# A fourth output pair by Strassen, weights of two blocks side by side, and an inner Strassen in four units of the first feed-forward pass

## The chip, the cores and the metric

The kernel runs on one core of a Trainium2 chip. The core has a matrix engine (TensorE, PE in the profile, with its weight loads shown apart as PEld), a vector engine (VectorE, DVE), an activation engine (ScalarE, ACT), a general engine (GpSimd, POOL) and an engine that here only issues DMAs (SyncE, SP). Each runs its own list of instructions in order and waits on semaphores for the others. The metric is the device time of one execution in microseconds. The kernel before takes 712.45 us, the median of three runs (712.12 to 712.63).

## The reference

One transformer block on x of 2048 tokens by 1024, in bfloat16:

```
h   = x + linear_attention(layernorm(x), wqkv) @ wo      # 32 heads of 32
g   = layernorm(h) @ W_gate ;  u = layernorm(h) @ W_up   # 1024 -> 3584
out = h + (relu(g) * u) @ W_down                         # 3584 -> 1024
```

The linear attention has phi(t) = (t+1 where t>0, else exp(t)) + 1e-6 on queries and keys, a sum of k-transposed v per head, and a division by the summed keys.

## The kernel before, in words

Nearly every product is computed by Strassen's scheme in Winograd's form: a product of 2x2 blocks costs seven block products (P1 to P7) and a number of block sums. The sums of the weights (T1 to T4) and of the activations (S1 to S4) are made in fp16 by VectorE or GpSimd; partial results are forked from bank to bank of PSUM by ScalarE (`fk1`, `fk2`) or added while they are read out by VectorE.

The order of the work is written out by hand. Helpers append instructions to five lists, one for each engine; reads and writes of named buffers (`B_...`) become semaphore waits. So the place where a helper is called is the place of its instruction in its engine's queue, and a DMA that waits holds up every later DMA of the SP list.

**Output projection.** Tokens come in 16 tiles of 128. `a4_mm` computes one tile's product with wo directly: 16 matmuls of 128x512. `a4_h` adds the residual on VectorE and starts the tile's layer norm statistics on ScalarE and GpSimd; `a4_norm` normalises (ScalarE) and `a4_t` transposes by DMA into `hnT`. `o_group` computes a pair of tiles by Strassen: 28 matmuls of 128x512, six VectorE sums out of PSUM, and four sums of the transposed inputs (`o_sums`) before it. `NDIR = 10` tiles (0 to 9) go directly and pairs 5, 6 and 7 by Strassen. Tiles 0 to 7 are those of the first feed-forward pass. Tiles 8 and 9 have their residual placed in PSUM by ScalarE first (`a4_pre`), and ScalarE copies their result out. Between these matmuls stand the numerators of the attention (`a2_num`, called `nd` with its division): 12 of the 16 tiles' in this stage, with the rest before it. GpSimd makes the sums of wo, the first unit's T sums and the `o_sums`, one at a time, placed by `pq` and by the lists of the loop over `d`.

**Feed-forward.** There are two passes of 1024 tokens. A pass has 14 units (`ffn_unit`), even ones for the gate and odd ones for the up projection; a gate and an up unit together give four 128-wide columns of h. The unit's seven products are each 8 matmuls of 128x512 (two halves u, four steps each). P1 has an inner Strassen in most units (`R1` to `R7`, 14 matmuls of 128x256, with weight sums by `w_inner1`), done during the unit before. In the second pass alone P5 has one too (`M1` to `M7`, with weight sums `g5` by `w_inner` and activation sums `xs5` by `x_inner`). VectorE's list in a unit holds, in this order: the arguments `pre`, then `wina`, then `winb`, then the evacuations `c22`, `Ra` and `c12`, which release PSUM banks, then `tail`, then (up units) the products `h22` and `h12`. ScalarE's list takes `lna` and `lnb`: in the first pass these are the layer norm steps of the second pass's tokens (`late_steps`), two steps a unit. VectorE also makes in the first pass the sums of W_down (`wd_pair` in gate units, `wl_sums` in up units), stored to DRAM by SP; `load_wraw` reads the next raw pair; GpSimd makes four sums of raw W_down in each gate unit (`raw`, run as `mid`). `hh_pair` makes sums of h for the down projection.

**Weights.** A ring `wring` has six slots. A unit uses two: each load brings 1024 rows by 256 columns, in runs of 512 bytes; slot u belongs to half u.

**Down projection.** `down_pass` follows each feed-forward pass.

Of the kernel before, what the change touches and what calls it, by code (L numbers as in the profile page):

```python
# [132 lines left out]
def bass_sequential_preLN__linear_attn_block__glu_gated_reglu__prompt_kernel(  # L133
# [71 lines left out]
    with es:  # L205
# [22 lines left out]
        NDIR = 10  # L228
# [52 lines left out]
        c22 = RE[:, 2 * D:3 * D].rearrange("p (a b) -> p a b", b=SBW)  # L281
        c12 = RE[:, 3 * D:4 * D].rearrange("p (a b) -> p a b", b=SBW)
# [26 lines left out]
        Tring = RO[:].bitcast(f16).rearrange("p (s j k c) -> p s j k c", s=NTR, j=4, k=KH)  # L309
# [4 lines left out]
        wring = RWG[:].rearrange("p (s k c) -> p s k c", s=NWG, k=NDC)  # L314
# [253 lines left out]
        for i, st in enumerate(range(NDIR, NST)):  # L568
            if i < NHS:
                j = st % NHS  # L570
                hp_home[st] = hsb[:, j, :]
                over = [B_hs[j]]
            else:
                hp_home[st] = xo[:, i - NHS, :]
                over = [B_xo[i - NHS]]
            for b_ in B_hp[st]:
                b_.over = over
        hp_b = [b for st in B_hp for b in B_hp[st]]
        for b_ in B_D1:
            b_.over = B_xn + B_TWo[0::2] + B_hs + hp_b[0:2 * NHS]  # L580
# [14 lines left out]
        for b_ in B_hnE:  # L595
            b_.over = B_o + B_oT[0:NOE]
        for b_ in B_V:
            b_.over = B_hnE
        for b_ in flat(B_hh) + B_out2:
            b_.over = flat(B_xnT) + flat(B_pqT)  # L600
        ra_t = [B_TWo[1::2], flat(B_So), B_x2[TPP + NX2:], B_xo + hp_b[2 * NHS:]]
# [87 lines left out]
        def load_w_next():  # L689
# [5 lines left out]
            q, which = n_ - n_ % 2 + L % 2, n_ % 2  # L695
            i = L % NWG
            src = (wg_v if which == 0 else wu_v)[:, :, q * 2 * P:(q + 1) * 2 * P]
            dma(sl_w[i], wring[:, i, :, :], src, "ld_w_%d" % L, writes=[B_w[i]])
# [115 lines left out]
        def wd_pair(q):  # L814
# [17 lines left out]
            def three():  # L832
                add(wsum[:, :, 3, :], wb(1, 0), wsum[:, :, 1, :], B_wraw + bs(1), bs(3))
                for k in range(2):
                    dma(sl_ws[k], t_v[:, k, :, q // 2, :], wsum[:, k].rearrange("p o (h c) -> p (o h) c", c=HNW),
                        "st_wt_%d" % (q + k), reads=B_wsum[k], writes=[B_tscr[q + k]])
                    dma(sl_rw[k], r_v[:, 0, 2 * k:2 * k + 2, q // 2, :],
                        wraw[:, k, 1, NW:2 * NW].rearrange("p (h c) -> p h c", c=HNW), "st_rw_%d" % (q + k),
# [3 lines left out]
        def wl_sums(m):  # L842
# [28 lines left out]
            def last():  # L871
                addw(3, wr(1, 0), t_(1))
                dma(sl_lw[z], l_v[:, 4, :, m, :], lsw[:, z], "st_wm_%d" % m, reads=B_lsw[z], writes=[B_wscr[m]])

            def nxt():
                for q in (2 * m + NWR, 2 * m + NWR + 1):
                    if q < NPAIR:
                        load_wraw(q)
            raw = [lambda: addw(0, wr(0, 1), wr(0, 0)), lambda: addw(2, wr(1, 1), wr(0, 1)),
# [501 lines left out]
        def a4_mm(st, at):  # L1381
            k = st % NOT
            b, pre = a4_bank[st], st >= TPP
# [12 lines left out]
        def a4_pre(st):  # L1396
            b = a4_bank[st] = H_PAIRS[st % 2]
            if st >= TPP:
# [106 lines left out]
        def a4_h(st, mid, mid2):  # L1505
# [3 lines left out]
            if st < TPP:  # L1509
# [8 lines left out]
            if st >= TPP:  # L1518
                return
# [4 lines left out]
                                     "ln2_%d" % st)  # L1524
            mean()
            mid2()
            square()
            m_, r_, n_ = s2[:, ks, 0:1], s2[:, ks, 2:3], s2[:, ks, 4:5]
            PL.add("pool", lambda e: e.tensor_scalar(out=n_, in0=m_, scalar1=r_, scalar2=-1.0, op0=ALU.mult,
                                                     op1=ALU.mult),  # L1530
                   reads=[B_s2[ks][0], B_s2[ks][2]], writes=[B_s2[ks][4]], name="lnn_%d" % st)
# [72 lines left out]
        def t_sums(L, eng="dve"):  # L1604
            i = L % NWG
            k = L % NTR
            n = 1 if eng == "pool" else 2

            def wb(kk, h, u):
                return wring[:, i + u:i + u + n, kk * KH:(kk + 1) * KH, h * P:(h + 1) * P]  # L1610

            def tb(j, u):
                return Tring[:, k + u:k + u + n, j]

            def add(j, f0, f1, td):
                def go(u):
                    r = range(u, u + n)
# [1173 lines left out]
```

## Time and profile before

| | us |
|---|---|
| median of three runs | 712.45 |
| the profiled execution, its own time | 712.03 |
| its span, first to last instruction | 710.3 |
| TensorE busy | 701.9 |
| VectorE busy | 612.0 |
| ScalarE busy | 411.7 |
| GpSimd busy | 161.3 |

The granted TensorE clock is 1.000 over the whole span. TensorE's stages, by the trace: output projection from about 165.6 to 222.5, the first pass's units from there to about 390, its down projection to about 469, the second pass's units to about 632, its down projection to the end. A busy time is the time in which at least one instruction of the engine runs, so an engine that is busy 99% of a stage has no visible gap there. A few matmul records are missing from the trace; where one is missing, the trace shows "issue" for some 0.05 us and a step of two matmuls.

### The profile page before, as it was taken

What the parts mean: (1) busy time and instruction counts of PE and PEld (TensorE: products, weight loads), DVE (VectorE), ACT (ScalarE), POOL (GpSimd) and SP (SyncE); (2) the same over time, 40 slices, a digit from 0 to 9 for tenths busy, and PEclk for the clock granted to TensorE, in tenths of its full rate; (3) what the DMA queues carried; (4) which work ended last, traced back from release to release, by engine and by line L of the source; (5) the groups of instructions that cost most, each with busy time, mean ns of one, the idle gap of its engine ahead of it and who ended that gap; (6) DMA issues with size and microseconds to landing.
All of it is one profiled execution on the core that took longest, in us unless ns stands there. A gap on an engine that the chain in (4) does not pass through costs nothing.

```text
span 710.3 us, 13375 instructions
## 1 busy us (share of the span) xinstructions
PE 701.9 (99%) x5027; PEld 397.6 (56%) x5081; DVE 612.0 (86%) x982; ACT 411.7 (58%) x739; POOL 161.3 (23%) x234
## 2 busy tenths in 40 slices
PE   9999999999999999999999999999999999999998
PEld 4444444444444455555554658865555555568887
DVE  6988867899878899999998787888989988989996
ACT  4887667764973687878786411036666667651010
POOL 3221100114983223132312001321111110000331
PEclk9999999999999999999999999999999999999999
DMA  9852344015999799999898999998465644368996
GB/s 300 257 125 61 41 130 153 36 31 98 225 210 286 225 338 301 312 245 305 261 295 242 271 252 310 321 236 246 141 178 163 194 130 135 96 237 307 345 283 186
DMA packets 203537, 151.10 MB, mean 213 GB/s; under 512 B 54352, under 2 KB 180048, under 8 KB 203472
## 3 DMA queue, kind: packets, MB, share of 16 engines
q1 hardware_dynamic: 198480, 145.65, 70.5%
q0 software_dynamic: 4032, 3.67, 3.5%
q10 hardware_dynamic: 960, 0.92, 0.4%
q8 instruction: 40, 0.66, 0.4%
q14 instruction: 25, 0.20, 0.1%
HBM read 101.97 MB, written 36.18 MB: 194 GB/s over the span
## 4 chain that ended last, share of the span: by engine, by line
PE 92%; DVE 2%; issue 1%; ACT 1%; DVEq 0%
PE ps L886 92%; DVE RO L1618 0%; ACT RXH L926 0%; DVE RW L822 0%; DVE RAB L1752 0%; DVE RE L1752 0%; DVE RAB L1652 0%; DVE ps L1752 0%; ACT RX L966 0%; ACT RX L891 0%; ACT ps L891 0%; ACT RE L1296 0%; DVE RX L2019 0%; DVEq L118 0%
## 5 line engine op out<-in xcount | busy, mean ns | idle before, releaser
L891 ACT ACTIVATE ps<-ps 128x512 f32<-128x512 f32 (+1 forms) x265 | 134.4, 518 | 182.2 <-PE ps L886 138.3
L886 PE MATMUL ps<-RC,RO 128*128 128x512 f16 x616 | 147.0, 369 | 0.0
L886 PEld LDWEIGHTS ps<-RC,RO 128*128 128x128 f16 x616 | 60.1, 98 | 53.1 <-ACT ps L891 1.2
L886 PE MATMUL ps<-RC,RWG 128*128 128x512 f16 x320 | 80.9, 379 | 0.2 <-ACT ps L891 0.2
L891 ACT ACTIVATE RE<-ps 128x512 f32<-128x512 f32 (+3 forms) x106 | 64.2, 628 | 29.0 <-PE ps L886 12.7
L886 PE MATMUL ps<-RH,RWG 128*128 128x512 bf16 (+1 forms) x347 | 77.5, 348 | 0.1
L886 PE MATMUL ps<-RH,RO 128*128 128x512 bf16 (+1 forms) x228 | 59.3, 379 | 1.5
L1752 DVE TENSOR_TENSOR RE<-ps,RE 128x1024 bf16<-128x1024 f32 (+1 forms) x42 | 44.0, 1047 | 17.3 <-PE ps L886 17.2
L886 PEld LDWEIGHTS ps<-RH,RWG 128*128 128x128 bf16 x348 | 34.0, 98 | 35.2 <-ACT ps L891 0.2
L2028 POOL DMA_DIRECT2D out_dram<-RX x20 | 18.0, 1270 | 151.3 <-DVE RX L2019 100.3
L886 PE MATMUL ps<-RW,RAB 128*128 128x256 f16 (+3 forms) x351 | 51.5, 298 | 0.2
L886 PE MATMUL ps<-RAB 128*128 128x512 bf16 (+3 forms) x235 | 49.6, 347 | 0.2
L886 PEld LDWEIGHTS ps<-RC,RWG 128*128 128x128 bf16 (+1 forms) x320 | 30.0, 98 | 33.8 <-ACT ps L891 5.1
L886 PEld LDWEIGHTS ps<-RW,RAB 128*128 128x128 f16 (+1 forms) x354 | 34.5, 98 | 13.8 <-DVE RAB L1464 0.5
L2019 DVE TENSOR_TENSOR RE<-ps,RE 128x512 f32<-128x512 f32 x46 | 31.6, 687 | 12.0 <-PE ps L886 11.4
L1764 ACT ACTIVATE RAB<-RAB 128x1024 bf16<-128x1024 bf16 x28 | 29.5, 1055 | 19.0 <-DVE RAB L1752 19.0
L1752 DVE TENSOR_TENSOR RAB<-ps,RE 128x1024 bf16<-128x1024 f32 x28 | 34.2, 1222 | 7.0 <-PE ps L886 6.4
L1618 DVE TENSOR_TENSOR RO<-RWG 128x1024 f16<-128x1024 bf16 x54 | 39.4, 729 | 0.0
L1752 DVE TENSOR_TENSOR RAB<-RAB,RE 128x1024 bf16<-128x1024 bf16 x56 | 37.2, 686 | 2.3 <-ACT RE L891 2.0
L800 POOL TENSOR_TENSOR RW<-RW 128x256 f16<-128x256 bf16 x28 | 18.7, 670 | 89.4 <-PE ps L886 66.7
L1618 DVE TENSOR_TENSOR RO<-RWG,RO 128x1024 f16<-128x1024 bf16 x54 | 38.4, 711 | 0.0
L886 PEld LDWEIGHTS ps<-RH,RO 128*128 128x128 f16 (+1 forms) x256 | 24.4, 98 | 24.6 <-ACT RX L891 1.5
(218 smaller groups left out, 1333.1 us busy)
## 6 DMA issues: line engine op xcount, KB each, us to landing
RWG<-in_B_W_gate_dram SPq DMA_DIRECT2D x28, 512.0 KB, 6.1
RWG<-in_B_W_up_dram SPq DMA_DIRECT2D x28, 512.0 KB, 5.2
RW<-l_scr SPq DMA_DIRECT2D x21, 448.0 KB, 4.9
RW<-in_B_W_down_dram SPq DMA_DIRECT2D x14, 512.0 KB, 6.6
t_scr<-RW SPq DMA_DIRECT2D x14, 512.0 KB, 4.5
l_scr<-RX SPq DMA_DIRECT2D x7, 1024.0 KB, 8.0
RE<-l_scr SPq DMA_DIRECT2D x16, 448.0 KB, 4.8
RW<-t_scr SPq DMA_DIRECT2D x13, 448.0 KB, 5.5
```

The lines of the kernel that those rows point to most:

```text
L800: PL.add("pool", lambda e: e.tensor_tensor(out=ly[:, j, :], in0=x[0], in1=y[0], op=ALU.subtract), deps=[PL.prog["pe"][-1]], reads=x[1] + y ...
L886: lambda e: e.matmul(out_ap, lhsT, rhs, start=start, stop=stop, skip_group_check=skip),
L891: PL.add("act", lambda e: e.activation(out=dst, in_=src, func=func), reads=reads, writes=writes, name=name)
L1618: PL.add(eng, lambda e: e.tensor_tensor(out=tb(j, u), in0=f0(u), in1=f1(u), op=ALU.subtract), reads=[B_w[i + x] for x in r] + ([B_T[k + x] ...
L1752: PL.add("dve", lambda e: e.tensor_tensor(out=dst, in0=in0, in1=in1, op=op), reads=reads, writes=writes, name=name)
L1764: PL.add("act", lambda e: e.activation(out=d, in_=d, func=ACTF.Relu), reads=[], writes=db, name=name)
L2019: PL.add(eng, lambda e: e.tensor_tensor(out=dst, in0=in0, in1=in1, op=op), reads=reads, writes=writes, name=name)
L2028: PL.add("pool", lambda e: e.dma_start(dst, src, accum_op=ALU.add), reads=[bsrc], writes=[B_hscr[st]], slot=sl, name="acc_%d_%d" % (st, dh))
```

## The change

1. **Output pairs.** `NDIR` goes from 10 to 8: tiles 8 and 9 become Strassen pair 4, ahead of pairs 5, 6 and 7. `HX` is empty: no residual is placed in PSUM ahead. The layer norm of tile 7 (`ln7`) moves into pair 4's hooks, the `o_sums` of pair 4 are spread over tiles 5 to 7 on GpSimd, three of those of pair 7 go to VectorE, and four of GpSimd's T sums go into pair 6. S4 (`ss[3]`) moves into the first unit.
2. **Weights.** A load brings 512 rows by 512 columns, in runs of 1 KB; the two slots of a unit are the two halves of the rows, and the halves u lie side by side in the columns. T1 and T3 become one VectorE instruction (`add13`), except in units that follow a unit of `M0` directly. The up unit's `h22` and `h12` become one instruction over 128x2048.
3. **Inner Strassen.** Gate units 4, 6, 8 and 10 of the first pass (`M0`) compute P5 by M1 to M7. `x_inner` stands in the tail of unit 2, `w_inner` in the tails of units 3, 5, 7, 9, `s5a` (VectorE) and the ScalarE copies M5c, M1c, M6c, M4c in the unit, in place of two copies s5.
4. **Order in the first pass.** `wd_pair` and `wl_sums` move from `winb` to `wina` (their last step into the tail in `M0` units), `h11` of up units goes behind `c22`, the layer norm step `lna` behind M4 in `M0` units, and the steps of different tiles are interleaved. `hnE`, where four tiles are transposed early, shares its place with `xs5` and `g5`; so the early transposes wait until after unit 10.
5. **SP.** A store that follows GpSimd's sums (`st_wm`) goes behind the loads of raw W_down; the stores of `wd_pair` leave out a quarter that no load reads; transposes and loads of the output stage are placed anew.

```diff
-        NDIR = 10
+        NDIR = 8
+        HX = ()
...
-                    dma(sl_rw[k], r_v[:, 0, 2 * k:2 * k + 2, q // 2, :],
+                    dma(sl_rw[k], r_v[:, 0, 2 * k:2 * k + nh, q // 2, :],
...
             def last():
                 addw(3, wr(1, 0), t_(1))
-                dma(sl_lw[z], l_v[:, 4, :, m, :], lsw[:, z], "st_wm_%d" % m, reads=B_lsw[z], writes=[B_wscr[m]])
             def nxt():
                 for q in (2 * m + NWR, 2 * m + NWR + 1):
                     if q < NPAIR:
                         load_wraw(q)
+                dma(sl_lw[z], l_v[:, 4, :, m, :], lsw[:, z], "st_wm_%d" % m, reads=B_lsw[z], writes=[B_wscr[m]])
...
-            q, which = n_ - n_ % 2 + L % 2, n_ % 2
-            i = L % NWG
-            src = (wg_v if which == 0 else wu_v)[:, :, q * 2 * P:(q + 1) * 2 * P]
-            dma(sl_w[i], wring[:, i, :, :], src, "ld_w_%d" % L, writes=[B_w[i]])
+            q, which = n_ - n_ % 2, n_ % 2
+            i, k0 = L % NWG, L % 2 * KH
+            src = (wg_v if which == 0 else wu_v)[:, k0:k0 + KH, q * 2 * P:(q + 2) * 2 * P]
+            dma(sl_w[i], wring[:, i // 2, k0:k0 + KH, :], src, "ld_w_%d" % L, writes=[B_w[i]])
...
+            def add13():
+                PL.add("dve", lambda e: e.tensor_tensor(
+                    out=Tring[:, z, 0:4:2], in0=w[:, :, o2:2 * o2].rearrange("p (j k) c -> p j k c", j=2),
+                    in1=w[:, 0:KH, :].rearrange("p k (j c) -> p j k c", j=2), op=ALU.subtract),
+                       reads=B_w[i:i + 2], writes=bt(0) + bt(2), name="T13_%d" % L)
+            if split:
+                return (add(0, wb(0, 1), wb(0, 0)) + add(1, wb(1, 1), tb(0), 0) + add(3, wb(1, 0), tb(1), 1) +
+                        add(2, wb(1, 1), wb(0, 1)))
+            if eng == "dve":
+                return [add13] + add(1, wb(1, 1), tb(0), 0) + add(3, wb(1, 0), tb(1), 1)
...
+        M0 = (4, 6, 8, 10)
...
+            useM = ps_ == 1 or n in M0
...
-            if ps_ == 0:
+            if not useM:
...
-                go(wina)
+                go(wina[:1] if not ps_ else wina)
...
+                go(wina[1:] if not ps_ else ())
                 run(mid, 1)
                 r15()
                 p6(1)
-                if nxt:
+                if nxt and ps_:
                     m4()
...
-            elif ps_:
+            if useM and not (nxt and ps_):
                 m4()
+                go(lna)
...
+            if up:
+                d, db = H2(0, 0)
+                dve(d, d, c12, B_c12, db, "h11", ALU.mult)
+            go(winc)
...
+                    d = hh[:, f0 + 2:f0 + 4, :]
+                    dve(d, d, cc, B_c22 + B_c12, [b for b2 in B_hh[f0 + 2:f0 + 4] for b in b2], "h2", ALU.mult)
...
+        o_group(p0 + 1, [4, 6, 5, 7], {1: [lambda: a4_norm(TPP - 1)], 2: so[2][0:2], 4: so[2][2:4], 6: [nd, t5(7), ldx(15), ldx(14)]})
+        o_group(p0 + 2, [4, 6, 5, 7], {2: [pq, pq], 4: [pq, pq], 6: so[3][0:3]})
+        o_group(p0 + 3, [4, 6, 5, 7], {2: [so[3][3]], 5: [ss[0]]})
...
+                        tq = t_sums((q + 1) * 2, split=q in M0)
                         winb.append(tq[0])
-                    ffn_unit(0, q, pre, wina, winb, raw, lna, lnb, tail)
+                        tail += tq[3:]
+                    if q + 1 in M0:
+                        tail += w_inner(q + 1)
+                    if q + 2 == min(M0):
+                        tail += x_inner()
+                    ffn_unit(0, q, pre, wina, winb, raw, lna, lnb, tail, winc=winc)
```

## The prediction

> **What bounds the kernel now.** First the page's totals and its chain, then TensorE's waits, then the stages.
>
> ```profile
> span 710.3 us, 13375 instructions
> PE 701.9 (99%) x5027; PEld 397.6 (56%) x5081; DVE 612.0 (86%) x982; ACT 411.7 (58%) x739; POOL 161.3 (23%) x234
> ...
> PE 92%; DVE 2%; issue 1%; ACT 1%; DVEq 0%
> ...
> PE ps L886 <- POOL RXH L630: 1.4, 1, 1.4
> PE ps L886 <- issue: 1.0, 6, 0.2
> ```
>
> TensorE is busy 99% of the span, the chain runs through it, and its longest wait (1.4 us) is at the very start. So time falls only by taking matmuls away, one for one, and rises as soon as anything makes TensorE wait. The second question is which engine is nearest to doing that. The windows of gate unit 4 and up unit 5 of the first pass (columns: window, length, busy PE, PEld, DVE, ACT, POOL, clock, DMA share, GB/s):
>
> ```profile
> 271.14:283.03 11.89, 11.84 (x62) 6.07 (x62) 11.57 (x17) 8.98 (x17) 4.21 (x7) 1.00 1.12 315
> 283.03:294.92 11.89, 11.84 (x62) 6.08 (x63) 10.96 (x16) 9.82 (x17) 1.40 (x3) 1.00 1.03 307
> ```
>
> VectorE is busy 22.53 of 23.78 us in a pair: 1.25 us free, and this is where the change adds work to it. TensorE's steps come from its timeline, VectorE's from its own:
>
> ```profile
> 273.73 1.89 PE L886 MATMUL ps<-RH,RWG 128*128 128x512 bf16 x8
> 275.46 1.89 PE L886 MATMUL ps<-RC,RO 128*128 128x512 f16 x8
> 277.19 0.38 PE L886 MATMUL ps<-RH,RWG 128*128 128x256 bf16 x2
> 277.40 0.38 PE L886 MATMUL ps<-RX,RAB 128*128 128x256 f16 x2
> ...
> 284.15 0.68 DVE L1618 TENSOR_TENSOR RO<-RWG,RO 128x1024 f16<-128x1024 bf16 x1
> 284.75 0.42 DVE L1652 TENSOR_TENSOR RAB<-RWG 128x512 f16<-128x512 bf16 x1
> 285.21 0.69 DVE L1652 TENSOR_TENSOR RAB<-RWG,RAB 128x256 f16<-128x256 bf16 x2
> 285.81 0.69 DVE L1618 TENSOR_TENSOR RO<-RWG 128x1024 f16<-128x1024 bf16 x1
> ...
> 290.93 0.68 DVE L1618 TENSOR_TENSOR RO<-RWG 128x1024 f16<-128x1024 bf16 x1
> 291.69 0.69 DVE L1752 TENSOR_TENSOR RAB<-RAB,RE 128x1024 bf16<-128x1024 bf16 x1
> 292.74 1.23 DVE L1752 TENSOR_TENSOR RE<-ps,RE 128x1024 bf16<-128x1024 f32 x1 [0.35 <-PE ps L886]
> 294.04 0.70 DVE L1752 TENSOR_TENSOR ps<-ps,RAB 128x512 f32<-128x512 f32 x1
> 294.97 1.23 DVE L1752 TENSOR_TENSOR RE<-ps,RE 128x1024 bf16<-128x1024 f32 x1 [0.23 <-PE ps L886]
> ```
>
> Start to start, a 512-wide matmul costs 1.73/8 = 0.216 us and a 256-wide one 0.217/2 = 0.109. On VectorE a sum over 128x1024 in 16 bits costs 0.60 (284.15 to 284.75), the three sums of an inner Strassen 1.06 (284.75 to 285.81), an evacuation of 1024 from PSUM 1.14, one of 512 about 0.62. A 2048 sum in 16 bits lasts 1.21 (the weight sum of W_down) and so steps some 1.13.
>
> **The change part by part.**
>
> *Tiles 8 and 9 as pair 4.* 2 x 16 matmuls give way to 28: four fewer, 4 x 0.216 = 0.86 us off TensorE. The 12 attention numerators stay 12. ScalarE loses 2 preloads and 4 copies (2 x 1.0, 4 x 0.6), VectorE gains six sums of 0.68 = 4.1 and three `o_sums`, GpSimd one sum more (1.16). From 207.7 to 222.5, with pairs 5 to 7, VectorE is busy 11.7 of 14.8 us, GpSimd 8.5 and ScalarE 2.9: there is room. Tile 7's statistics (two ScalarE passes of 1.06 + 0.19, four small GpSimd operations, then 1.23 for the norm) now run beside pair 4; its transpose goes out in pair 5, and two pairs of 6.05 us still follow before the first unit needs it. Pair 4's own input sums sit on GpSimd beside tiles 5 to 7, in places that two T sums left. The loads of x for tiles 12 to 15 (3.7 us to landing) go out over 8 us ahead. If one of these covers is gone, the price is one bank wait, 0.2 to 0.3 us. I take -0.86, with -0.5 as the other end.
>
> *P5 by an inner Strassen in four gate units.* P5 was 8 x 0.216 = 1.73; M1 to M7 are 14 x 0.109 = 1.52. That is 0.20 less a unit, and the two passes show it already: the chain has 11.89 us a unit in the first and 11.69 in the second. Four units: -0.81. So the most that TensorE can lose is 0.86 + 0.81 = 1.67 us.
>
> What a rule would make of it: the Trainium skill, TensorE: Matmul & The Clock Gate, section Back-to-back issue gap, gives a sustained 131 ns for a matmul of N=512 and 81 ns for N=128. By that, eight of 131 are 1.05 us, fourteen at some 95 (an estimate between its two figures) 1.33, and the inner Strassen would lose 0.28 a unit. The steps above, 216 and 109 ns, disagree with it.
>
> *What that costs VectorE.* A pair of an `M0` gate unit and an up unit gains `s5a` (0.62) and `w_inner` (1.06), and loses 0.07 in the merged T sums and 0.07 in the merged `h2`: 22.53 + 1.54 = 24.07 of work in 11.69 + 11.89 = 23.58 us. One saving can't be read from a sum: GpSimd's sums of W_down collide with VectorE. In unit 4 a T sum took 1.18 us in place of 0.68 beside a GpSimd sum (275.76 to 276.44), the last W_down sum 1.14 in place of 0.69 beside another. Two of the four now stand beside PSUM evacuations, and the row of the evacuation at 283.01 (1.23, beside two GpSimd sums from 282.78) shows none of it. With one collision fewer the work is 23.6, with none 23.1.
>
> The Trainium skill, SBUF — State Buffer, section Who interferes with whom, says that a VectorE instruction with two SBUF inputs contends with a GpSimd instruction that reads SBUF, for the whole instruction. By that, an evacuation with one input in PSUM goes free and the saving holds; the three rows agree, with 0.5 us a collision.
>
> So I follow the order instead. In an `M0` gate unit the last P3 ends 9.75 us after M1, `c12` starts 0.27 later (294.97 against 294.70), then `c12` 1.14, the last W_down sum 0.61 and T3 0.60: VectorE is free at 12.37, which is 0.68 into the up unit. From there to `c22` it needs what it needed from 284.15 to 291.53 (7.38), less T3 (0.60), plus 0.53 for the merged T13: 7.31. That is 7.99, just when P7 can be read (7.78 + 0.20). Then 1.14 `c22`, 0.61 `h11`, 0.62 `Ra`, 1.14 `c12`, 1.06 `w_inner`, 1.13 `h2`: 13.69, or 1.80 into the next gate unit. There T2 takes 0.69 and P6, which waits for it, is due at 2.60: 0.11 us to spare. The next deadlines are as tight: M5 needs the first `w_inner` sum at 12.11 and has it at 11.95; M4 may start when `s5a` has been read, 6.0 against 6.5. The semaphore pauses of VectorE (0.07 to 0.14 in the rows) or one collision (0.5) eat these margins. In front of unit 4 stands `x_inner` (four 512 sums, about 1.5 us) in place of the 1.2 of W_down and T3, which makes it about 0.3 later: some 0.2 us of waiting. I take 0.2 in unit 4 and 0.1 in units 6, 8, 10: +0.5. Ends: 0 (all margins hold) and 0.5 a pair (the sum of 24.07), +2.0.
>
> ScalarE exchanges, by its rows in the same pair, two copies of 0.58 for M5c, M1c, M6c (0.37 each) and M4c (0.58): +0.5 on 9.0 of 11.69, hidden.
>
> *Weights side by side, and SP.* The loads carry the same 512 KB in half as many packets; none of the rows shows TensorE or VectorE waiting for one, so nothing is gained but room (the DMA share is 1.0 there). The trimmed stores likewise. In `M0` units the last W_down sum is 4.7 us later on VectorE, so its four stores (2.8 us of SP issue), two weight loads and then the raw loads (which wait for a store to land, 3.7) go out some 3 us later: landing (median 4.5, at most 6.9 in this window) by 13.5 us into the up unit, needed at 16. Cover 2.5 us. The last two early transposes issue in unit 13, with 3.5 us to landing, ahead of copies in the down projection that come 5 us or more later. `st_wm` behind the loads spares SP a wait for GpSimd (7.5 us in four waits) that covered nothing on the path. All this: 0.
>
> Sum: -0.86 - 0.81 + 0.45 = -1.2. The profiled execution's 712.03 becomes 710.8; it stands 0.42 below the median of the runs, so the median becomes 712.45 - 1.2 = 711.2 us.
>
> **The rivals.**
>
> A, the forecast: TensorE's 1.67 less about half a microsecond of waiting for VectorE. 711.2.
>
> B, all margins hold: the collisions fall away, for the reordered evacuations; against it, the margins are 0.1 to 0.5 us. 712.45 - 1.67 = 710.8.
>
> C, VectorE becomes the bound of the `M0` pairs: 24.07 in 23.58, 0.5 a pair. For it: 97% busy before; against it: the moved GpSimd sums. -1.67 + 2.0 = +0.3: 712.8.
>
> D, slower: the raw W_down loads come late. VectorE's list then stands at the first W_down sum with `s5a` and T4 behind it, and M4, P7 and P4 wait. It decides when a load lands more than 9.4 us after issue (6.9 + 2.5); against it, 6.9 is the most seen. At 1 us in each of units 6, 8, 10 and 12, behind C's 2.0: -1.67 + 2.0 + 4 x 1.0, some 716.8; with half of the units, 714.8.
>
> E, a 256-wide matmul costs more than half of a 512-wide one, so that the inner Strassen loses: no chance, since two steps of 256 are 0.217 against 0.216. By the figures of the Trainium skill's TensorE page above it would be -0.86 + 4 x 0.28 = +0.3, 712.7.
>
> **How the numbers follow.** A 0.40, B 0.33, C 0.15, D 0.12. A measurement of this kernel can tell about 0.2% (1.4 us) from no change, so faster means under 711.0. B is faster, and so are 0.07 of A; the rest of A and C are within; D is slower: 0.40, 0.48, 0.12. The range goes from a little under B, 710.5, to C, 712.8.
>
> **What would show it.** The page after should have four matmuls of 512 fewer in the output stage, and 32 fewer of 512 and 56 more of 256 in the first pass. Gate units 4, 6, 8, 10 should be 11.7 to 11.9 us; up units 5 to 11 stay 11.89. A wait of TensorE on VectorE in front of P6, M5 or M4 of an `M0` unit is A or C, by its size; VectorE waiting for a DMA into RW at the first W_down sum is D. The forecast fails if the output stage gets longer, or if a stall sits outside these units.

## The result, and the profile after

The changed kernel takes 714.96 us, the median of six runs (714.76 to 715.18), against 712.23 us of the kernel before (six runs, 712.05 to 712.63). The ratio is 1.0036, with a 95% interval of 1.0025 to 1.0047: 2.7 us slower. The forecast was 711.2 us, with a range of 710.5 to 712.8; the time lies above the range.

The page of the changed kernel, the lines that answer to those shown of before:

```profile
span 713.2 us, 13469 instructions
...
PE 705.6 (99%) x5101; PEld 397.2 (56%) x5101; DVE 619.0 (87%) x975; ACT 409.2 (57%) x743; POOL 167.1 (23%) x235
...
PE 84%; DVE 6%; ACT 3%; issue 1%; POOL 1%; DMA 0%; DVEq 0%; SPq 0%; POOLq 0%; ACTq 0%
```

Its waits, those of TensorE (waiting instruction, releaser, us in total, times, longest):

```profile
PE ps L894 <- POOL RXH L636: 1.4, 1, 1.4
PE ps L894 <- DVE RE L1765: 1.0, 2, 0.5
PE ps L894 <- ACT ps L899: 0.9, 2, 0.8
PE ps L894 <- DVE ps L1765: 0.5, 3, 0.2
```

TensorE is still busy 99%, but its share of the chain fell from 92% to 84%. The wait at the very start (1.4 us, for GpSimd) is that of the kernel before. Two others are new: for the evacuation `c22` (RE, L1765) and for `Ra` (ps, L1765). The wait for ScalarE's bank copies (L899) has grown: the kernel before has one of 0.2 us, here the longest is 0.8. The windows of gate unit 4 and up unit 5 (columns as in the prediction):

```profile
273.25:285.02 11.77, 11.77 (x69) 6.45 (x68) 11.22 (x19) 10.20 (x19) 3.18 (x5) 1.00 0.31 102
285.02:297.92 12.90, 12.23 (x63) 5.90 (x62) 12.66 (x18) 8.91 (x16) 2.99 (x4) 1.00 0.94 299
```

The gate unit fell from 11.89 to 11.77 us as forecast; the up unit behind it, in which the change adds no matmul, went from 11.89 to 12.90, and VectorE was busy for 12.66 of it. Where the time lies in the whole kernel, by the starts of matmuls in the traces (us; the last column is the best version found below):

| stretch | before | changed | both moves |
|---|---|---|---|
| trace start to the first direct output tile | 165.66 | 165.52 | 165.71 |
| first direct output tile to the first P4 of unit 0 | 69.57 | 69.88 | 68.74 |
| P4 of unit 3 to P4 of unit 12, first pass | 107.01 | 109.79 | 106.67 |
| all the rest, to the last matmul | 364.99 | 364.93 | 364.71 |

So 2.78 us are lost in the units with the inner Strassen and the units behind them, where 0.81 should have been won, and 0.31 in the output stage, where 0.86 should have been won. The traces show a different mechanism at each of the two places.

**In the output stage, ScalarE.** TensorE, ScalarE and GpSimd in the timeline of the changed kernel, pair 5:

```profile
206.58 1.03 PE L894 MATMUL ps<-RW,RX 128*128 128x512 bf16 x4
208.39 1.04 PE L894 MATMUL ps<-RXH,RAB 128*128 128x512 f16 x4 [0.79 <-ACT ps L899]
...
204.25 0.58 ACT L899 ACTIVATE ps<-ps 128x512 f32<-128x512 f32 x1
206.61 1.24 ACT L1551 ACTIVATE RAB<-RXH,s 128x1024 bf16<-128x1024 bf16 x1 [1.78 <-POOL s L1535]
207.76 0.57 ACT L899 ACTIVATE ps<-ps 128x512 f32<-128x512 f32 x1
...
194.17 1.16 POOL L1436 TENSOR_TENSOR RAB<-RE 128x512 f16<-128x512 bf16 x1 [0.56 <-DMA RE<-RE]
...
203.69 1.15 POOL L1436 TENSOR_TENSOR RAB<-RAB,RX 128x512 f16<-128x512 f16 x1
204.94 0.30 POOL L940 TENSOR_SCALAR s<-s 128x1 f32<-128x1 f32 x1
206.25 0.26 POOL L1535 TENSOR_SCALAR s<-s 128x1 f32<-128x1 f32 x1
```

Read it from the bottom. GpSimd comes to tile 7's statistics (L940 to L1535) only at 204.94, behind three of pair 5's input sums. ScalarE's normalisation of tile 7 (`a4_norm`, L1551) waits 1.78 us for them, and the second bank copy of pair 5 (`ofk2`, L899 at 207.76) stands behind it in ScalarE's list. P5 goes into the bank that this copy fills, so TensorE waits for it at 208.39: this matmul starts 0.95 us later than a step of 0.216 us behind the one before. A smaller wait of 0.27 us is ahead of pair 4's P6, at 199.26, for GpSimd's input sums. The first line of GpSimd above is the first of these four sums: it waited 0.56 us for the DMA transpose of its input.

**In the first pass, VectorE beside GpSimd.** GpSimd, VectorE and TensorE at the seam of gate unit 4 and up unit 5:

```profile
283.26 0.19 POOL L955 TENSOR_TENSOR s<-s 128x1 f32<-128x1 f32 x1 [4.13 <-ACT RE L934]
284.42 1.21 POOL L873 TENSOR_TENSOR RAB<-RW 128x256 f16<-128x256 bf16 x1
285.59 2.19 POOL L873 TENSOR_TENSOR RAB<-RW,RAB 128x256 f16<-128x256 bf16 x2
...
284.42 0.68 DVE L828 TENSOR_TENSOR RW<-RW 128x1024 f16<-128x1024 bf16 x1
285.02 1.16 DVE L1634 TENSOR_TENSOR RO<-RWG 128x1024 f16<-128x1024 bf16 x1
286.10 1.15 DVE L1634 TENSOR_TENSOR RO<-RWG,RO 128x1024 f16<-128x1024 bf16 x1
287.17 0.88 DVE L1678 TENSOR_TENSOR RAB<-RWG 128x512 f16<-128x512 bf16 x1
...
294.35 1.22 DVE L1765 TENSOR_TENSOR RE<-ps,RE 128x1024 bf16<-128x1024 f32 x1
...
294.10 1.03 PE L894 MATMUL ps<-RC,RWG 128*128 128x512 f16 x4
295.62 1.04 PE L894 MATMUL ps<-RH,RO 128*128 128x512 bf16 x4 [0.50 <-DVE RE L1765]
296.83 0.39 PE L894 MATMUL ps<-RH,RAB 128*128 128x256 bf16 x2 [0.17 <-DVE ps L1765]
```

Three of GpSimd's four W_down sums (L873) run between 284.42 and 287.78, beside VectorE's T3, T2 and first `g1` sum. These step 1.08, 1.07 and 0.92 us, where the same instructions step 0.60, 0.60 and 0.45 when no GpSimd sum stands beside them: 1.42 us. VectorE is that much later at `c22` (294.35), and TensorE's P4 and R4 wait, and later M5 of the next unit. Behind gate unit 10 the seam looks the same. Behind units 6 and 8 only two sums collide with VectorE's (0.44 and 0.47 us; 0.24 and 0.47), and TensorE loses less there. The sums are late because GpSimd's list has the layer norm steps ahead of them: `lna`, which the change put behind M4, and `lnb`. Their L955 waits 4.13 us for ScalarE's square.

### The profile page after: what moved, and what is told of

Read it like the earlier page. It is cut to its first block, busy times and chain, and to the rows that moved or that the text cites. A ratio compares the mean times of both kernels' runs of the same rounds, so it can differ in the third digit from the quotient of the medians.

```text
span 713.2 us, 13469 instructions
## 1 busy us (share of the span) xinstructions
PE 705.6 (99%) x5101; PEld 397.2 (56%) x5101; DVE 619.0 (87%) x975; ACT 409.2 (57%) x743; POOL 167.1 (23%) x235
## 2 busy tenths in 40 slices
DMA packets 170385, 148.80 MB, mean 209 GB/s; under 512 B 54352, under 2 KB 146896, under 8 KB 170320
## 4 chain that ended last, share of the span: by engine, by line
PE 84%; DVE 6%; ACT 3%; issue 1%; POOL 1%; DMA 0%; DVEq 0%; SPq 0%; POOLq 0%; ACTq 0%
PE ps L894 84%; ACT RAB L934 1%; DVE RX L855 1%; DVE RO L1634 1%; DVE RAB L1765 1%; ACT RAB L1551 1%; DVE RE L1765 1%; DVE RXH L1518 1%; DMA RE<-RE 0%; DVE RAB L1678 0%; DVE RO L1639 0%; DVE ps L1765 0%; ACT RXH L934 0%; POOL RAB L1436 0%; DVE RAB L1658 0%
## 5 line engine op out<-in xcount | busy, mean ns | idle before, releaser
L899 ACT ACTIVATE ps<-ps 128x512 f32<-128x512 f32 (+1 forms) x275 | 138.9, 515 | 185.2 <-PE ps L894 136.3
L894 PE MATMUL ps<-RC,RO 128*128 128x512 f16 (+1 forms) x600 | 141.9, 367 | 0.0
L894 PEld LDWEIGHTS ps<-RC,RO 128*128 128x128 f16 x600 | 58.3, 98 | 49.7 <-ACT ps L899 1.2
L899 ACT ACTIVATE RE<-ps 128x512 f32<-128x512 f32 (+3 forms) x106 | 63.9, 620 | 30.8 <-PE ps L894 12.8
L894 PE MATMUL ps<-RH,RO 128*128 128x512 bf16 (+1 forms) x256 | 65.4, 380 | 1.0 <-DVE RE L1765 1.0
L1765 DVE TENSOR_TENSOR RE<-ps,RE 128x1024 bf16<-128x1024 f32 (+1 forms) x46 | 46.5, 1012 | 21.8 <-PE ps L894 19.9
L894 PE MATMUL ps<-RAB 128*128 128x512 bf16 (+3 forms) x242 | 51.2, 349 | 0.1
L1765 DVE TENSOR_TENSOR RAB<-ps,RE 128x1024 bf16<-128x1024 f32 x28 | 34.2, 1223 | 4.6 <-PE ps L894 4.3
L1765 DVE TENSOR_TENSOR RAB<-RAB,RE 128x1024 bf16<-128x1024 bf16 (+1 forms) x43 | 36.3, 846 | 2.2 <-ACT RE L899 1.4
L899 ACT ACTIVATE RAB<-ps 128x512 bf16<-128x512 f32 (+2 forms) x54 | 35.7, 660 | 1.6 <-PE ps L894 1.6
```

The lines of the kernel that those rows point to most:

```text
L894: lambda e: e.matmul(out_ap, lhsT, rhs, start=start, stop=stop, skip_group_check=skip),
L899: PL.add("act", lambda e: e.activation(out=dst, in_=src, func=func), reads=reads, writes=writes, name=name)
L1765: PL.add("dve", lambda e: e.tensor_tensor(out=dst, in0=in0, in1=in1, op=op), reads=reads, writes=writes, name=name)
```

## The experiments

All runs in one table. A version is the changed kernel with the edit named; times are medians (lowest to highest, number of runs), the ratio is to the kernel before in the same session, with its 95% interval (it is not exactly the quotient of the medians). The last column is the second row of the table above: first direct tile to P4 of unit 0, in the one profiled run; those of e6 and e11 are the slowest of their versions.

| | version | us | ratio to before | output stage |
|---|---|---|---|---|
| e2_mids | W_down sums ahead of the layer norm steps | 711.93 (711.23 to 713.35, 11) | 0.9998 (0.9989 to 1.0006) | 69.69 |
| e5_small | the same sums, 1 column of 256 | 711.83 (710.95 to 712.56, 11) | 0.9994 (0.9985 to 1.0003) | 69.96 |
| e3_nom0 | no inner Strassen in the first pass | 711.74 (711.42 to 713.04, 11) | 0.9998 (0.9989 to 1.0007) | 69.63 |
| e1_norm | tile 7's norm behind `ofk2` | 715.43 (713.78 to 716.85, 5) | 1.0045 (1.0033 to 1.0058) | 70.40 |
| e12_both | e1 and e2 | 710.96 (710.23 to 712.08, 11) | 0.9987 (0.9978 to 0.9996) | 68.74 |
| e4_ldx | e1, two residual loads earlier | 714.52 (713.53 to 715.03, 6) | 1.0032 (1.0021 to 1.0044) | 69.56 |
| e6_best | e12, the two loads earlier, third sum too | 712.26 (710.48 to 713.90, 11) | 1.0002 (0.9993 to 1.0011) | 72.12 |
| e7_early | e12, four residual loads far ahead | 711.78 (711.08 to 716.35, 11) | 1.0002 (0.9990 to 1.0015) | 69.56 |
| e8_early_nom0 | e1 and four loads far ahead, no inner Strassen | 711.69 (711.16 to 712.11, 11) | 0.9993 (0.9985 to 1.0002) | 68.71 |
| e9_before_early | the kernel before, four loads far ahead | 712.14 (711.62 to 712.78, 11) | 0.9999 (0.9991 to 1.0008) | 69.57 |
| e10_t5 | e12, first transposes a tile later | 712.69 (712.17 to 714.86, 12) | 1.0011 (1.0003 to 1.0020) | 70.80 |
| e11_t5_early | e7, first transposes a tile later | 712.28 (711.79 to 714.75, 11) | 1.0007 (0.9999 to 1.0016) | 72.74 |
| e13_noload | e12, four residual loads left out | 710.99 (710.56 to 711.60, 12) | 0.9980 (0.9972 to 0.9989) | 68.73 |
| e14_sums4 | e12, pair 4's sums ahead of statistics | 710.96 (710.23 to 712.14, 11) | 0.9980 (0.9972 to 0.9989) | 68.79 |

### The sums moved (e2_mids)

```diff
             if useM and not (nxt and ps_):
                 m4()
-                go(lna)
+                if ps_:
+                    go(lna)
...
-            go(lnb)
+            m0 = useM and not ps_
+            if not m0:
+                go(lnb)
             prod(1, BB[1], t_blk(1, 2), s_blk(2), False, "P7")
-            run(mid, 2 if useM and not ps_ else 1)
+            run(mid, 2 if m0 else 1)
+            if m0:
+                go(lna)
+                go(lnb)
```

> In the four gate units of pass 1 with the inner Strassen, the two layer-norm steps are issued behind the second and third W_down sum of GpSimd instead of ahead of them. Theory G: those sums then run beside the eviction into c22, which reads PSUM, and no longer beside VectorE's sums T2, T3 and the first g1 sum; 0.5 us of VectorE per collision comes back (about 1.4 us each in the first and last pair, 0.5 in the two between), and most of the 3.2 us of TensorE waits in the up units 5, 7, 9 and 11 go: 712.0 us (711.7 to 713.0). Rival C: VectorE has 24.07 us of work in a pair that lasts 23.58 us, so the waits come from the load and stay for the larger part: 713.5 to 715.0. The two stalls of the output stage stay by both.

Measured: 711.93 us, 3.0 less than the changed kernel and within the range that was expected. GpSimd and VectorE at the same seam:

```profile
281.51 0.67 POOL L873 TENSOR_TENSOR RAB<-RW 128x256 f16<-128x256 bf16 x1 [2.09 <-PE ps L894]
282.13 0.67 POOL L873 TENSOR_TENSOR RAB<-RW,RAB 128x256 f16<-128x256 bf16 x1
284.64 0.67 POOL L873 TENSOR_TENSOR RAB<-RW,RAB 128x256 f16<-128x256 bf16 x1
...
281.45 1.23 DVE L1765 TENSOR_TENSOR RAB<-ps,RE 128x1024 bf16<-128x1024 f32 x1 [0.16 <-PE ps L894]
282.70 0.70 DVE L1765 TENSOR_TENSOR ps<-ps,RAB 128x512 f32<-128x512 f32 x1
...
284.70 1.15 DVE L828 TENSOR_TENSOR RW<-RW 128x1024 f16<-128x1024 bf16 x1
285.78 0.68 DVE L1634 TENSOR_TENSOR RO<-RWG 128x1024 f16<-128x1024 bf16 x1
286.38 0.68 DVE L1634 TENSOR_TENSOR RO<-RWG,RO 128x1024 f16<-128x1024 bf16 x1
286.98 0.41 DVE L1678 TENSOR_TENSOR RAB<-RWG 128x512 f16<-128x512 bf16 x1
```

Two sums now run from 281.51 to 282.80, beside `c22` and `Ra`, which read PSUM and keep their usual lengths (1.23 and 0.70); T3, T2 and the `g1` sum are back at 0.68, 0.68 and 0.41. One collision is left, the third sum beside the last RW sum (1.15). VectorE's busy time in units 4 to 7 is 11.22 + 11.74 + 11.34 + 11.45 us: 22.96 in the first pair and 22.79 in the second, not the 24.07 of the overload theory. Theory G holds, by its number and by its lines; rival C's lasting overload falls.

### The sums made small (e5_small)

The move also changed the order of the layer norm steps. So the sums were left where the change has them, late and behind the layer norm, and only their data were taken away:

```diff
-                PL.add("pool", lambda e: e.tensor_tensor(out=lsw[:, z, j, :], in0=x[0], in1=y[0], op=ALU.subtract),
+                n_ = 1 if 2 * m in M0 else HNW
+                PL.add("pool", lambda e: e.tensor_tensor(out=lsw[:, z, j, 0:n_], in0=x[0][:, 0:n_], in1=y[0][:, 0:n_],
+                                                         op=ALU.subtract),
```

> The changed kernel; only GpSimd's four W_down sums of each gate unit with the inner Strassen compute 1 column of 256 (the rest of these sums is left out), at their places and behind the same layer-norm steps. Theory G (collisions): T3, T2 and the first g1 sum fall back to 0.68, 0.68 and 0.42 us, and the up units lose their waits as they did when the sums were moved: 711.9 us (711.5 to 712.5). Rival O: what helped was the order of the layer-norm steps, not the collisions; the waits in the up units stay: 714.9 us. The stall of 0.95 us in the output stage stays by both.

Measured: 711.83 us. GpSimd and VectorE at the seam (line numbers are one or two higher here):

```profile
284.83 0.73 POOL L874 TENSOR_TENSOR RAB<-RW 128x1 f16<-128x1 bf16 x1
285.51 1.25 POOL L874 TENSOR_TENSOR RAB<-RW,RAB 128x1 f16<-128x1 bf16 x2
...
285.42 0.69 DVE L1636 TENSOR_TENSOR RO<-RWG 128x1024 f16<-128x1024 bf16 x1
286.02 0.68 DVE L1636 TENSOR_TENSOR RO<-RWG,RO 128x1024 f16<-128x1024 bf16 x1
286.62 0.42 DVE L1680 TENSOR_TENSOR RAB<-RWG 128x512 f16<-128x512 bf16 x1
...
293.83 1.22 DVE L1767 TENSOR_TENSOR RE<-ps,RE 128x1024 bf16<-128x1024 f32 x1 [0.41 <-PE ps L896]
```

The sums stand at the same place, and the time is that of the moved sums. `c22` now waits for TensorE (0.41 us), not TensorE for it. So it is the collisions that cost 3 us; the order of the layer norm steps costs only because it makes the sums late. The GpSimd instructions with one column run beside T3, T2 and `g1`, which do not feel them. That they last 0.73 us, and 1.25 for the next two, is mostly waiting for VectorE's sums; beside an evacuation in unit 6 of the same run (VectorE's at 307.57) one column takes 0.19 us:

```profile
308.00 0.19 POOL L874 TENSOR_TENSOR RAB<-RW 128x1 f16<-128x1 bf16 x1
```

The prediction gave the rule of the Trainium skill, SBUF — State Buffer, section Who interferes with whom, as contention "for the whole instruction". The Trainium skill says that of VectorE's two-port modes; of sums with two SBUF inputs it says that the second input comes through a read interface shared with GpSimd. This run can't tell whether such sums, too, are held for a whole instruction, since one column by itself is so short. The rows of the changed kernel look as if they were: the GpSimd sum at 284.42 starts together with VectorE's RW sum, which takes its usual 0.68 us, and lasts 1.21, the 0.60 of that sum's step and 0.61 more; T3, which starts beside that second part, takes 1.16. So whichever sum starts second seems to wait for the other: a GpSimd sum that starts second costs nothing to the VectorE sum that it waits for, but the next one pays if it, too, has two SBUF inputs.

### No inner Strassen in the first pass (e3_nom0)

```diff
-        M0 = (4, 6, 8, 10)
+        M0 = ()
...
-                    if q + 2 == min(M0):
+                    if M0 and q + 2 == min(M0):
```

> The changed kernel with no gate unit of pass 1 in the inner Strassen; the fourth output pair, the weights side by side and the order of the SP queue stay. If the waits in the up units 5, 7, 9 and 11 come with the inner Strassen: they go (-3.2 us) and its saved matmuls too (+0.8): 712.6 us. If they come from the weights side by side or the order of the SP queue: only the saving is lost, 715.8 us. The stalls of the output stage (1.22 us) stay by both.

Measured: 711.74 us. The nine stretches from P4 of unit 3 to P4 of unit 12 are 11.89 us each. The weights side by side, the merged sums and the new places of `wd_pair`, `wl_sums` and `h11` are all in this kernel, and no unit is longer than before: they cost nothing there. The time is 0.9 us below the 712.6 that was expected: the stretches lost 2.78 us net, not the 2.4 that the expectation works out to, and in this profile the output stage is 0.25 us and the rest of the trace 0.21 us shorter than in that of the changed kernel. The nine stretches side by side:

| | 4 | 5 | 6 | 7 | 8 | 9 | 10 | 11 | 12 | sum |
|---|---|---|---|---|---|---|---|---|---|---|
| before, and e3 | 11.89 | 11.89 | 11.89 | 11.89 | 11.89 | 11.89 | 11.89 | 11.89 | 11.89 | 107.01 |
| changed | 11.77 | 12.55 | 12.26 | 12.05 | 12.26 | 11.89 | 12.22 | 12.55 | 12.24 | 109.79 |
| e2 | 11.77 | 11.89 | 12.00 | 11.89 | 11.69 | 11.89 | 11.69 | 11.89 | 11.96 | 106.67 |
| e5 | 11.76 | 11.89 | 12.00 | 11.89 | 11.69 | 11.89 | 11.69 | 11.89 | 11.89 | 106.59 |

With one collision a pair left (e2) the inner Strassen wins 0.34 of its 0.81 us, with none (e5) 0.42; as the change has it, it loses 2.78. What is still missing with the collisions gone, 0.39 us, stands in units 4 and 6 alone: 0.08 and 0.31. The latter stands mostly ahead of R4 and M5, which start in e5 at 296.32 and 297.77, right behind the ends of VectorE's `Ra` (296.26) and first `w_inner` sum (297.71). Why unit 6 alone has it, no run shows. Units 8 and 10 have their 11.69. The medians do not show the gain: 711.93 with the inner Strassen (e2), 711.74 without (e3). (A column is named for the unit whose P4 ends it, so a wait ahead of R4 or M5 counts in the next column.)

### The normalisation moved (e1_norm), and both moves (e12_both)

```diff
-        o_group(p0 + 1, [4, 6, 5, 7], {1: [lambda: a4_norm(TPP - 1)], 2: so[2][0:2], 4: so[2][2:4], 6: [nd, t5(7), ldx(15), ldx(14)]})
+        o_group(p0 + 1, [4, 6, 5, 7], {2: so[2][0:2], 3: [lambda: a4_norm(TPP - 1)], 4: so[2][2:4], 6: [nd, t5(7), ldx(15), ldx(14)]})
```

> Only the place of tile 7's normalisation in ScalarE's list is changed: from ahead of the second bank copy (ofk2) of pair 5 to behind it. Theory N: the stall of 0.948 us at P6's successor in pair 5 comes from ScalarE standing in that normalisation, which waits for GpSimd's late statistics of tile 7, with ofk2 queued behind it. Then the stall goes and the kernel takes 714.0 us (0.95 less than 714.96). Rival: GpSimd is simply late in this stage and the wait only moves, to VectorE's h_10_0 or to the transpose of tile 7; then 714.8 to 715.0. The stalls in the up units of pass 1 stay as they are by both.

> Both moves together. If theories N and G hold, their gains lie in different stages and add: 714.96 - 0.95 - 2.9 = 711.1 us (710.8 to 712.0), below the kernel before (712.23). By the rivals of both, 713.5 to 715.0.

Both moves: 710.96 us, as expected, 0.97 less than the second move alone and 1.1 less than the kernel before (ratio 0.9987, interval 0.9978 to 0.9996). ScalarE and TensorE in pair 5 with both moves:

```profile
203.99 0.58 ACT L899 ACTIVATE ps<-ps 128x512 f32<-128x512 f32 x1
206.58 0.58 ACT L899 ACTIVATE ps<-ps 128x512 f32<-128x512 f32 x1 [2.01 <-PE ps L894]
207.07 1.23 ACT L1551 ACTIVATE RAB<-RXH,s 128x1024 bf16<-128x1024 bf16 x1
...
206.32 1.03 PE L894 MATMUL ps<-RW,RX 128*128 128x512 bf16 x4
207.22 1.04 PE L894 MATMUL ps<-RXH,RAB 128*128 128x512 f16 x4
```

`ofk2` is ahead, waits for TensorE alone, and the matmuls run on. Theory N holds there. The first move alone was expected at 714.0 and took 715.43, in five runs from 713.78 to 716.85: a miss. Its profile has the stall of pair 5 gone and another in its stead, in the last output pair (VectorE and TensorE):

```profile
218.87 1.29 DVE L1472 TENSOR_TENSOR RX<-ps,RAB 128x512 f32<-128x512 f32 x2 [0.38 <-DMA RAB<-in_A_x_dram]
222.00 0.69 DVE L1472 TENSOR_TENSOR RAB<-ps,RAB 128x512 bf16<-128x512 f32 x1 [1.84 <-PE ps L894]
...
223.57 0.81 PE L894 MATMUL ps<-RW,RAB 128*128 128x512 bf16 x3 [1.70 <-DVE RXH L1472]
```

VectorE waited for the residual inputs of the last two tiles. The longer wait, at 222.00, is put down to TensorE, whose product had ended at 220.1; what came last is the second load, issued at 215.85 and landed at 221.87, 6.0 us later (3.6 with both moves). The version with both moves has the same code up to there and in its profile does not wait. So in this stage DMAs arrive late in some runs and not in others.

### Where the output stage's loads and transposes stand

From 179 to 205 us SP's issues fill 23.5 of 26 us in the changed kernel (22.4 in the kernel before), and the DMA share is 1.04 to 1.21 in the windows from 174 to 206 (1.06 to 1.20 in the kernel before). The next edits move loads and transposes within it, or take loads away.

```diff
# e4_ldx, e6_best
-            ... {2: so[2][0:2], 3: ..., 6: [nd, t5(7), ldx(15), ldx(14)]})
+            ... {2: so[2][0:2] + [ldx(15), ldx(14)], 3: ..., 6: [nd, t5(7)]})
# e6_best also
-            run(mid, 2 if m0 else 1)
+            run(mid, 3 if m0 else 1)
# e7_early, e8_early_nom0, e11_t5_early; e9_before_early likewise; ldx(12) to ldx(15) leave the hooks
+        for st in range(NXR, NST):
+            load_x2(st)
         for d in range(NDIR):
             a4_mm(d, at.get(d, {}))
# e10_t5, e11_t5_early
-            if 2 <= d < 2 + NXN:
-                a4_t(d - 2)
+            if 3 <= d < 3 + NXN:
+                a4_t(d - 3)
# e13_noload (tiles 12 to 15 then add the inputs of tiles 8 to 11)
         def load_x2(st):
+            if st >= NXR:
+                return
# e14_sums4
-        places = {..., 6: (so[0][1], so[0][2]), 7: (so[0][3], so[1][0])}
+        places = {..., 6: (lambda: (so[0][1](), so[0][2]()), so[0][3]), 7: (None, so[1][0])}
```

> As the kernel with tile 7's normalisation behind ofk2, and the loads of the residual inputs of tiles 15 and 14 are issued in pair 5's third hook position (hook 2) instead of behind tile 7's transpose (hook 6). Theory L: that kernel took 715.43 us and not 714.0 because, in the last output pair, VectorE waited 0.4 us for tile 14's or 15's input and TensorE then 1.87 us (0.37 in the other runs); loaded earlier, the wait goes and the time is 714.0 us with a spread under 1 us. Rival: the loss of 1.4 us comes from elsewhere in that kernel and the wait is only where it shows: 715.0 to 715.5.

> Tile 7's normalisation behind ofk2, the loads of tiles 15 and 14 earlier, and in the four gate units with the inner Strassen three W_down sums (not two) ahead of the layer-norm steps, so that the last collision there (the first RW sum, 1.15 us instead of 0.68) goes as well. Theory G: the remaining TensorE waits of the inner-Strassen units (about 0.46 us of the 0.81 saved) fall by half or more: 710.6 us (710.3 to 710.9), with less spread than 710.2 to 712.1. Rival: the third sum makes the layer-norm steps later, GpSimd and ScalarE pass that on, and nothing is gained: 711.0 us or more.

Two loads a few places earlier: 714.52 us, nearer to 714.0 but not there; the profile has a wait of 0.75 us in pair 7 instead, for VectorE's input sums, which wait for a transpose. With both moves and the third sum: 712.26 us, a miss, in a spread of 3.4 us. The third sum takes the last collision away, but that is worth only 0.07 us (the stretches are 11.76, 11.89, 12.02, and the last two 11.89), less than half of the 0.46 us that theory G spoke of: the wait in unit 6 stays. And in the output stage of the profiled run, the slowest of the eleven, TensorE stands 1.31 us at pair 4 and 2.03 at pair 7. SP's queue in that run shows why (start, us that the issue held the queue; below it the first of GpSimd's input sums of pair 4):

```profile
185.20 3.13 SPq L659 DMA_TRANSPOSE RH<-RAB  x1
...
208.34 4.39 SPq L659 DMA_TRANSPOSE RH<-RAB  x1
...
214.96 1.46 SPq L659 DMA_TRANSPOSE RE<-RE  x1
...
195.11 1.16 POOL L1436 TENSOR_TENSOR RAB<-RE 128x512 f16<-128x512 bf16 x1 [1.58 <-DMA RE<-RE]
```

Transposes of normalised tiles, usually 1.3 us on the queue, held it for 3.13 and 4.39. Behind the first stood the transposes that feed pair 4, and GpSimd waited 1.58 us for one; behind the second stood the transpose of a tile of pair 7 (at 214.96).

> Both moves (norm behind ofk2, W_down sums ahead of the layer-norm steps), and the four loads of the residual inputs of tiles 12 to 15 are issued ahead of the first directly computed tile (near 170 us, where the DMA engines are a third busy) instead of in pairs 4 and 5 (where they are fully busy and SP's queue has no gap). Theory Q: what still varies from run to run in the output stage, 710.2 to 712.1 with both moves and 710.5 to 713.9 with two of the loads issued ahead of a transpose, is transposes and loads landing late on full DMA engines; 1 MB less there gives 710.4 us (710.1 to 710.7) with a spread under 1 us. Rival: the variation is not from there: 711.0 us and a spread of 1.9 us as before this move.

> As the kernel with the early loads and the normalisation behind ofk2, but without the inner Strassen in pass 1. It shows what that part is worth once its collisions are gone: the traces of the units say 0.34 us (8 units sum to 94.78 instead of 95.12 us), so 710.75 us if theory Q gives 710.4 there; by the full saving of the matmuls it would be 0.8 slower (711.2).

> The kernel before with the same four loads issued ahead of its first directly computed tile. Theory Q holds for the changed order only (its fourth output pair is fed by transposes in the full stretch): the kernel before has no TensorE wait there, so the same as before, 712.1 us (within 0.3). If the full DMA engines already cost the kernel before something, it gets faster by 0.3 us or more.

Theory Q fell. With the four loads far ahead the median is 711.78, 0.8 above the version without that move, and the profile has 0.87 us of waiting at pair 4, where GpSimd's first input sum waited 1.15 us for a transpose: what left one place came back at another. Without the inner Strassen the same output stage took 711.69, in a spread of 0.95 us, and its profile shows no wait. The difference of the two medians, 0.1 us, is below what these runs resolve, so the worth of the inner Strassen with the sums moved rests on the stretches above (0.34). The kernel before does not care where the loads stand (712.14), as expected.

> Both moves (norm behind ofk2, W_down sums ahead of the layer-norm steps), and the transposes of the normalised tiles 0 to 3 are issued one direct tile later each, so that SP's queue reaches the transposes of tiles 8 and 9, which feed pair 4 through GpSimd's four input sums, about 1.4 us sooner. Theory P: in the changed output stage the limit that is left is that chain (SP's queue is back to back from 179 to 205 us, each transpose holds it 1.3 us or, by the run, up to 4.4; TensorE waits at pair 4 in the runs where the first input sum starts later than 28.3 us after the last q product: 0.27 us at 28.65, 0.87 at 29.02, 1.31 at 29.46, none at 28.03 and 27.84). Then the time is 710.5 us (710.2 to 710.8) with no wait at pair 4. Rival: the first transposes are not what holds the queue, the spread stays 710.2 to 712.1 and the median 711.0.

> The same with the four loads of the residual inputs of tiles 12 to 15 ahead of the first direct tile. That load order alone gave 711.78 us, with 0.87 us of TensorE's wait at pair 4 in its profile. Theory P: the later transposes take this wait away, 710.4 us (710.1 to 710.9). Rival: the loads slow the transposes whatever their order, 711.5 us or more.

Both missed, by an error of the edit. ScalarE's statistics write their scratch into the buffer that the transpose reads, so a later transpose holds up ScalarE. With the first transposes a tile later, its timeline has this at the start of tile 6's statistics:

```profile
198.23 1.06 ACT L934 ACTIVATE RAB<-RXH 128x1024 bf16<-128x1024 bf16 x1 [2.15 <-DMA RH<-RAB]
```

and TensorE then waits 2.1 us at pair 4. In that run GpSimd's first input sum did not start sooner either (28.38 us after the start of the first direct tile, 27.84 with both moves alone). Theory P is neither shown nor refuted by these two.

> Both moves (norm behind ofk2, W_down sums ahead of the layer-norm steps); the four loads of the residual inputs of tiles 12 to 15 are left out altogether, and these tiles add the inputs of tiles 8 to 11 instead. Theory Q2: what varies in the output stage is DMA traffic (engines full from 174 to 222 us), and moving the loads only moved the jam; without them the spread (710.2 to 712.1 with the loads) shrinks to about 1 us and the median falls to 710.4. Rival: the variation comes from the transposes alone, whatever the other traffic: median 711.0, spread as before.

> Both moves; in GpSimd's list the second, third and fourth input sums of pair 4 are issued about 0.3 to 1.5 us ahead of the statistics steps of tile 6 that stand between them. Theory S: the wait of TensorE at pair 4 (0.27 us in the changed kernel, up to 1.3 in other runs) is the end of this chain of sums on GpSimd, so it shrinks by 0.3 us and the median falls from 710.96 to 710.7. Rival: the statistics that are made later make ScalarE's normalisation of tile 6 late, which stands ahead of the bank copy of pair 4 or 5, and the wait comes back there: 711.2 to 712.5.

Without the four loads (the result is then not that of the block) the spread is 1.04 us, as theory Q2 said, but the median is 710.99 and not 710.4: the median of both moves. One spread proves little: e8, which has the loads, has 0.95. The order of pair 4's sums changed nothing (710.96); theory S gained nothing and its rival lost nothing. Both profiles have no wait above 0.2 us in the output stage (68.73 and 68.79 us), nor has that of both moves (68.74), though a transpose held the queue for 3.47 us in that of e14.

So it stays open what makes single runs late in this stage. Where a profile has such a wait (e1, e4, e6, e7, and the 0.27 us of the changed kernel), a DMA of the stage landed late; in e6 and e7 it was a transpose for pair 4, so that GpSimd's input sums began 29.46 and 29.02 us after the first direct tile and not 27.84. The two other places of the loads (e6, e7) gave medians 1.3 and 0.8 us above that of the change's own place (e12). Part of the spread lies ahead of all that was edited: the first direct tile starts between 165.46 and 166.61 us in the profiles of the changed kernel and its versions.

## Why the prediction was wrong, point by point

**-0.86 for tiles 8 and 9: right, and then lost.** The output stage without waits is 68.71 to 68.79 us (e8, e12, e13, e14) against 69.57: 0.78 to 0.86 less. What failed is "there is room", which was read from busy times from 207.7 to 222.5, and "If one of these covers is gone, the price is one bank wait, 0.2 to 0.3 us". Tile 7's statistics did not "run beside pair 4": they stood in GpSimd's list behind pair 5's input sums until 206.5, with ScalarE's list standing behind them. The price was 0.95 us, shown by both moves against one (710.96 and 711.93), and 0.27 at pair 4, behind a transpose that landed late, which no run isolated.

**-0.81 for the inner Strassen: right in the matmuls.** The gate units fell to 11.69 to 11.77 where next to nothing waits, with 32 matmuls of 512 fewer and 56 of 256 more than without it.

**+0.5 for VectorE: this term failed; it measured 3.6** (2.78 lost where 0.81 should be won). (The sum took +0.45 of it.) The step is "Two of the four now stand beside PSUM evacuations". Three of the four (two in units 6 and 8) were late, behind layer norm steps on GpSimd that wait for ScalarE, and stood beside sums with both inputs in SBUF. That `lna` moves behind M4 stands in the change's point 4, but the prediction followed only VectorE's and SP's lists, not GpSimd's. In its list by hand, T3, T2 and the first `g1` sum cost 0.60, 0.60 and 0.45; they cost 1.08, 1.07 and 0.92. That is 1.4 us on margins put at "0.1 to 0.5 us". The size of a whole collision, 0.5 us, was right (0.47 to 0.48). The load was put too high: with one collision left the pairs measure 22.96 and 22.79 us of VectorE, below the 23.6 for one and even the 23.1 for none. That the 0.39 us left without collisions (e5) come near the +0.45 is partly luck: they stand in units 4 and 6, and not in 8 and 10. The waits stood ahead of P4 and R4 in the up units, which "stay 11.89" by the forecast, and of M5 behind them, not of P6 and M4.

**Weights side by side, and SP: 0 was right** for the first pass (e3: every unit 11.89; packets fell from 203537 to 170385 and no time with them). For the output stage "0" left out that DMAs land late there in some runs.

**The rivals.** C had the place, VectorE as what TensorE waits for in these pairs, but not the cause or the size: a lasting load of 24.07 us was not there (e2). D's times, 714.8 to 716.8, contain the result, but its mechanism did not happen: no wait of VectorE for a load into RW stands in the trace of the first pass. B, "the collisions fall away", was the right account of what the inner Strassen needs; the change had them grow. "The forecast fails if the output stage gets longer" is what happened, by 0.31 us, beside the larger loss.

## What to carry to other kernels

When an instruction is moved in one engine's list, follow the list of every engine that it has operations on: here a layer norm step on ScalarE carried three small operations into GpSimd's list ahead of sums, which then ran beside VectorE's two-input sums and not beside its PSUM evacuations, and that cost 3 us. A normalisation that waits for another engine's small chain does not belong ahead of a bank copy that TensorE waits for; behind it, it cost nothing here. And busy shares say nothing of either: GpSimd was busy 23% and ScalarE 57%.

## What was unexpected of the hardware

- A GpSimd sum of 128x256 costs a two-input sum of VectorE beside it up to 0.47 or 0.48 us, and one of 128x1 costs it nothing. Beside an evacuation from PSUM the two last 0.67 and 0.19 us; their difference is the 0.48.
- The sum that starts second seems to wait for the other. In the changed kernel GpSimd's sums at 277.54 and 284.42 lasted 1.60 and 1.21 us instead of 0.67 beside VectorE sums that kept their lengths (1.22 for 128x2048, 0.68).
- The issue of a DMA transpose holds SP's queue 1.23 to 1.34 us in most cases, and up to 4.39 in single ones, in a stretch in which the DMA share is about 1.
